# An attention and feed-forward block: which queue carries the maxima rows, the sums and the split weights, who computes the norm factors, and where the transposes stand

## The chip, the cores and the metric

The kernel runs on one core of a Trainium2 chip. Its time is the device time of one execution in microseconds. An execution can also be recorded by the hardware profiler, and every view quoted below comes from one such profiled execution. The engines have short names there: PE is TensorE's matmul row and PEld its weight loads, DVE is VectorE, ACT is ScalarE, POOL is GpSimd, SP is SyncE. A name that ends in q (SPq, ACTq, POOLq) is that engine's sequencer, which issues transfers.

## The reference

One transformer block on x of 2048 rows by 512 columns, with a modulation computed from a vector c:

```
mod = silu(c) @ w_mod                        # six vectors of 512: sa, ca, ga, sb, cb, gb
h = layernorm(x) * (1 + ca) + sa
q, k, v = split(h @ wqkv)                    # 32 heads of 16 columns
o = softmax(q k^T / 4) v                     # per head, 2048 by 2048 scores
x = x + ga * (o @ wo)
h = layernorm(x) * (1 + cb) + sb
x = x + gb * ((silu(h @ w_gate) * (h @ w_up)) @ w_down)      # 1792 hidden columns
```

All of it is float32. The kernel keeps that precision by splitting an operand into a rounded high part and a low rest and adding three products: high by high, high by low, low by high.

## The kernel before

The work falls into three stages. In the first, the rows of x are normalized, modulated, turned and multiplied with wqkv; queries and keys go to the DRAM buffers `qd` and `kd` in parts, and the values stay in `v_flat`. The second is the attention loop with most of the rest of the block laid into it. The third finishes what is left after the last score.

**Units and steps.** The 2048 queries are four chunks of 512, the 32 heads are eight groups of four. A *unit* is one chunk with one group, so there are 32 units, and every eight units end a chunk. A unit has 16 *steps*, one for each tile of 128 keys; the loop has 512 steps. In a step `score` (L496) runs once per head: one matmul of 128 keys by 512 queries into a PSUM bank and an exp on ScalarE into one of 13 tiles `pt_`. The product with the values, `pv_step` (L506), is done in two halves of 256 columns per step and follows the scores some steps later; it sums into one bank for the whole unit, and a column of ones in `v_flat` makes the row sums beside the products.

**Maxima.** The softmax needs each row's maximum before its scores are exponentiated. `max_one` (L466) computes the scores of a later unit once more in the other orientation and VectorE reduces each of these 128 by 512 results (L477). This runs 19 steps ahead of the scores (LEAD = 20), one such matmul beside each score matmul. When a unit's maxima are complete, `max_parts` (L479) joins and negates them on VectorE, and one step later `max_rows` (L488) turns them on TensorE, copies them on ScalarE and sends them as two extra rows into that unit's query operand `qop` with two transfers that ScalarE issues. They have to be there when the unit's first score starts.

**A unit's end.** `close_unit` (L816) runs when the last product of a unit has been issued, which is in the first step of the next unit. The output tile is copied from PSUM by ScalarE, in two halves inside plain steps. Then come, in order: `out_a` (the row sums go from the copied tile to the column tile `dn`), `out_b` two steps later (reciprocal on VectorE, then `dn` to DRAM), `out_r` three steps later (each head's row back from DRAM, repeated over 32 partitions, into `rb`), `out_c` four steps later (product on GpSimd, then to `o_dr`). All four transfers are on GpSimd's queue. At the end of a chunk `begin` loads its x and the output projection's weights at once, `load_o` (L647) fetches the chunk's outputs at five steps and `split_o` splits them at six.

**Keys and queries.** Three key buffers `kop` and three query buffers rotate. `before` (L827) reloads the keys of the unit after next at step 0 of a unit (two transfers of 768 KB) and its queries at step 1 (two of 192 KB), on SyncE's queue.

**Filling.** `plain` (L895) runs steps in groups of three pairs of a score and a maximum matmul, each group followed by a share of the products with the values. `filled` (L908) runs two steps and lays twelve ticks of other TensorE work between their pairs, LONG and SHORT being the two patterns. For each of the first three chunks the order is: plain steps up to `STARTS[ci]`; the output projection in four filled groups; six plain steps during which `scaled` (L796) issues `norm_scale` and `normalize` piece by piece from a side generator; two filled groups without work of their own, each followed by eight transposes (`turned`, L682) and two `modulate`; and then the feed-forward jobs, each `gate_up` in two filled groups and each `down` in one. `norm_scale` (L661) finds 1/sqrt(variance) of four row tiles by four Newton steps on tiles of 128 by 4, on VectorE; `normalize` (L678) applies it on ScalarE. After the third chunk's norm, REST = 30 plain steps come before its jobs, and seven of its jobs (KEEP) are left for the third stage. The fourth chunk's block is done there as well, with the last unit's way through `out_a` to `load_o` ahead of its output projection.

**Weights.** `split_weights` (L572) loads the raw weights of wo, gate, up and down, scales and splits them on GpSimd, and stores the parts to DRAM. It advances by one piece at two of every five steps from the start of the loop (L855). Its loads and stores are on SyncE's queue, as are the later loads of the parts, `load_gu` (L637, one gate/up tile of 1 MB, one job ahead) and `load_wd`.

The order of the work is written out by hand: each engine and each queue takes its instructions in the order in which this program emits them, and waits are set where a tile's reader or writer requires it.

## Time and profile before

| | |
|---|---|
| median of three runs | 2095.19 us (2092.72 to 2097.70) |
| the profiled execution | 2095.88 us |
| its span | 2093.7 us |
| TensorE matmuls, share of the span | 94% |
| VectorE | 75% |
| ScalarE | 60% |
| GpSimd | 20% |
| granted clock of TensorE, mean | 0.958 |

A page of the profile gives such shares; a view of windows gives, for a stretch of time, how long an engine (or one line's instructions) was busy, how many instructions it had and what clock was granted. A view of groups has one row per line, engine and kind of operation, with the busy time, the mean of one in ns, and the idle time of the engine just before them with what ended it. The view in order of time has one row per instruction, with its start, its length, and in brackets the idle time before it and who ended it. The chain of waits follows the instruction that ended last back to what released it, step by step.

### The profile page before, as it was taken

The numbers are of one execution on the slowest core, as the hardware profiler recorded it, in microseconds if no ns is written. First come the engines' busy times: TensorE is split into PE (matmuls) and PEld (weight loads), VectorE is DVE, ScalarE is ACT, GpSimd is POOL, SyncE is SP. The second block draws the span as 40 slices with busy tenths as digits, with TensorE's granted clock in tenths as the row PEclk, the third lists the DMA queues.
The fourth block names the chain that finished last, engine by engine and source line by source line (L and its number), as shares of the span: only waits on it lengthen the run. The fifth ranks groups of instructions, "written<-read, shape, count | busy, mean of one in ns | idle before, by whom it ended". The sixth has DMA issues, their size and how long they took to land.

```text
span 2093.7 us, 40510 instructions
## 1 busy us (share of the span) xinstructions
PE 1960.2 (94%) x16836; PEld 1185.0 (57%) x16836; DVE 1579.0 (75%) x2663; ACT 1251.8 (60%) x2306; POOL 422.4 (20%) x463
## 2 busy tenths in 40 slices
PE   7999989999998999999999999999999999998798
PEld 5765434444455666665446666664454466666687
DVE  6468978889897888888887888887887988831333
ACT  4224767778766666666766666666766766673100
POOL 2001254442022111111202111111202011122321
PEclk9998989999998999999999999999998999999899
DMA  8773575665453344443443443433532334332542
GB/s 295 250 235 90 125 217 158 222 169 126 115 130 64 93 116 104 109 110 90 130 110 84 105 108 90 133 90 69 130 70 49 90 89 118 135 117 96 201 181 101
DMA packets 84924, 267.69 MB, mean 128 GB/s; under 512 B 16540, under 2 KB 29340, under 8 KB 64060
## 3 DMA queue, kind: packets, MB, share of 16 engines
q1 hardware_dynamic: 67012, 239.82, 42.0%
q0 software_dynamic: 16576, 24.76, 3.7%
q8 instruction: 132, 2.16, 0.4%
q10 hardware_dynamic: 1152, 0.52, 0.1%
q14 instruction: 52, 0.43, 0.1%
HBM read 201.85 MB, written 62.13 MB: 126 GB/s over the span
## 4 chain that ended last, share of the span: by engine, by line
PE 63%; DMA 12%; DVE 10%; issue 6%; ACT 4%; POOL 3%; ACTq 1%; SPq 0%; POOLq 0%; DVEq 0%
PE bank L517 16%; PE bank L707 14%; PE bank L502 13%; DMA dn<-o 8%; DVE mx L477 7%; PE bank L715 6%; PE bank L475 6%; PE bank L207 6%; DMA rb<-d_dr 1%; DMA mid<-in_B_w_gate 1%; ACTq L494 1%; POOL wgu L581 0%; PE bank L687 0%; POOL mid L761 0%; DMA d_dr<-dn 0%
## 5 line engine op out<-in xcount | busy, mean ns | idle before, releaser
L477 DVE TENSOR_REDUCE mx<-bank 128x1 f32<-128x512 f32 x2048 | 1310.2, 685 | 223.1 <-PE bank L475 174.6
L502 PE MATMUL bank<-qop,kop 50*128 50x512 f32 x2048 | 810.1, 447 | 50.3 <-ACT pt__6239 L504 2.2
L475 PE MATMUL bank<-kop,qop 48*128 48x512 f32 x2048 | 821.0, 452 | 31.8 <-DVE mx L477 30.0
L502 PEld LDWEIGHTS bank<-qop,kop 50*128 50x128 f32 x2048 | 369.5, 191 | 385.6 <-issue 79.1
L475 PEld LDWEIGHTS bank<-kop,qop 48*128 48x128 f32 x2048 | 365.2, 191 | 73.5 <-DVE mx L477 51.3
L707 PE MATMUL bank<-act,wgu 64*128 64x512 f32 x1872 | 306.4, 393 | 0.3 <-DVE m L759 0.2
L707 PEld LDWEIGHTS bank<-act,wgu 64*128 64x128 f32 x1872 | 204.6, 187 | 33.9 <-DVE m L759 3.3
L707 PE MATMUL bank<-wd,mid 64*128 64x512 f32 x912 | 154.4, 398 | 1.0 <-POOL mid L761 0.4
L760 POOL CAST mid<-m 128x512 fp32r<-128x512 f32 x56 | 34.3, 612 | 482.2 <-DVE m L759 203.8
L707 PEld LDWEIGHTS bank<-wd,mid 64*128 64x128 f32 x912 | 100.2, 188 | 19.3 <-DVE m L759 3.2
L753 ACT ACTIVATE th<-bank 128x512 f32<-128x512 f32 x56 | 33.5, 598 | 123.8 <-PE bank L715 123.8
L757 DVE SCALAR_TENSOR_TENSOR q<-th,bank 128x512 f32<-128x512 f32 x56 | 38.2, 682 | 82.4 <-ACT th L753 82.4
L529 POOL DMA_DIRECT2D dn<-o x32 | 22.7, 711 | 384.0 <-ACT o L523 182.7
L207 PE MATMUL bank<-hT,wqs 128*128 128x512 f32 x384 | 95.4, 399 | 3.6 <-DVE prt L366 2.4
L207 PEld LDWEIGHTS bank<-hT,wqs 128*128 128x128 f32 x384 | 70.4, 188 | 26.0 <-issue 5.9
L772 DVE TENSOR_TENSOR x<-bank,x 128x512 f32<-128x512 f32 x84 | 54.1, 683 | 31.0 <-PE bank L707 21.0
L761 POOL TENSOR_TENSOR mid<-m,mid 128x512 fp32r<-128x512 f32 x56 | 72.2, 1289 | 4.6
L715 PE MATMUL bank<-wd,mid 128*128 128x512 f32 x216 | 56.7, 419 | 12.5 <-DVE q L757 7.8
L545 POOL TENSOR_TENSOR on<-o,rb 128x512 f32<-128x512 f32 x32 | 41.0, 1282 | 135.4 <-DMA rb<-d_dr 135.4
L534 POOL DMA_DIRECT2D d_dr<-dn x32 | 18.2, 568 | 198.6 <-DVE dn L533 198.6
L715 PEld LDWEIGHTS bank<-wd,mid 128*128 128x128 f32 x216 | 43.0, 201 | 24.7 <-DVE q L757 8.3
L366 DVE TENSOR_TENSOR prt<-bank,prt 128x512 fp32r<-128x512 f32 x32 | 22.0, 689 | 45.0 <-ACT prt L364 43.0
(6258 smaller groups left out, 5286.1 us busy)
## 6 DMA issues: line engine op xcount, KB each, us to landing
wgu<-gu_dr SPq DMA_DIRECT2D x48, 1024.0 KB
kop<-kd SPq DMA_DIRECT2D x62, 768.0 KB
wd<-wd_dr SPq DMA_DIRECT2D x28, 1024.0 KB
gu_dr<-wgu SPq DMA_DIRECT2D x14, 1024.0 KB
qop<-qd SPq DMA_DIRECT2D x64, 192.0 KB
kd<-prt SPq DMA_DIRECT2D x16, 512.0 KB
qd<-prt SPq DMA_DIRECT2D x16, 512.0 KB
rb<-d_dr POOLq DMA_DIRECT2D x32, 256.0 KB, 5.0
```

The source lines that it names most:

```text
L207: nc.tensor.matmul(pt, lhs(a, k), rhs(b, k), start=(n == 0), stop=(n == 3 * nk - 1))
L475: nc.tensor.matmul(pm, qop[u][rows, s, qt * P:(qt + 1) * P], kop[u % 3][rows, s, kc * CW:(kc + 1) * CW], start=True, stop=True)
L477: nc.vector.tensor_reduce(mx[u][:, b, s, qt, kc:kc + 1], pm, op=ALU.max, axis=AX.X)
L502: nc.tensor.matmul(sp, kop[u % 3][rows, h // 2, kt * P:(kt + 1) * P], qop[u][rows, h // 2, :], start=True, stop=True)
L517: nc.tensor.matmul(pv[u][32 * h:32 * h + 32, cols], v_flat[:, e0:e0 + 32], p_[h][:, cols], start=(kt == 0 and half == 0), stop=(kt == 15), ...
L545: nc.gpsimd.tensor_mul(on, o, rb)
L707: nc.tensor.matmul(outs[e], lhs(e, a, k)[rows], rhs(b, k)[rows], start=(ph == 0 and j == 0), stop=(ph == 1 and j == z))
L715: nc.tensor.matmul(outs[e], lhs(e, a, k), rhs(b, k), start=(j == 0), stop=(j == z))
L757: nc.vector.scalar_tensor_tensor(q, th, 1.0, outs[0], op0=ALU.add, op1=ALU.mult)
L760: nc.gpsimd.tensor_copy(mid[:, 0, :], m32)
L761: nc.gpsimd.tensor_sub(mid[:, 1, :], m32, mid[:, 0, :].bitcast(F32))
L772: nc.vector.tensor_add(ch.x2[:, t, :], outs[e], ch.x2[:, t, :])
```

## The change

- The two transfers of the maxima rows move from ScalarE's to SyncE's queue.
- The transfers of `out_a`, `out_b` and `out_r` move from GpSimd's to SyncE's queue; the one of `out_c` stays on GpSimd's, one step later. For the last unit all are on ScalarE's queue, issued one behind the other, and the product is on VectorE.
- Keys and queries of the unit after next are both loaded at step 6 of a unit instead of steps 0 and 1. `begin`, `load_o` and `split_o` come 6, 7 and 9 steps after a chunk's end instead of 0, 5 and 6.
- The weights' loads and stores move from SyncE's to GpSimd's queue; a piece is advanced every fourth step, two raw loads are kept ahead, and stores are issued as soon as their tile is made.
- The output tile is copied in one piece in plain steps too, and what remains of a group's products after a unit's end is put off to the next group.
- `norm_scale` leaves three operations on VectorE and puts the other 18 on the engine it is given, GpSimd inside the loop; `normalize` is on GpSimd inside the loop. Both are issued at once ahead of nine plain steps (NORM).
- The 16 transposes of a chunk are laid four by four into the last four groups of three further plain steps, each with its `modulate`, in the banks that the maxima use.
- Projections start six, eight and four steps later (STARTS), REST falls from 30 to 24.
- In the third stage the kept gate/up jobs go ahead of the kept down jobs, 36 of their matmuls beside the last unit's sums and 36 ahead of the norm factors, which stay on VectorE there. One more tile is lent to a `mid` of the last kept job.
- An exp on a small tile is put at the end of the first stage.

```diff
-REST = 30
-STARTS = (141, 267, 399)
+REST = 24
+NORM = 9
+STARTS = (147, 275, 403)
...
     sm.finish()
+    nc.scalar.activation(pa.tile([P, 1], F32, name="warm1"), eps_t, AF.Exp)
...
-            nc.scalar.dma_start(qop[u][64 * b + KR:64 * b + KR + 2].bitcast(F32), mr[16 * b:16 * b + 16].bitcast(F32))
+            nc.sync.dma_start(qop[u][64 * b + KR:64 * b + KR + 2].bitcast(F32), mr[16 * b:16 * b + 16].bitcast(F32))
...
-        if kt == 15 and by_halves:
-            nc.scalar.copy(o_[u][:, cols], pv[u][:, cols])
-        elif kt == 15 and half:
+        if kt == 15 and half:
             nc.scalar.copy(o_[u], pv[u])
...
-        nc.gpsimd.tensor_mul(on, o, rb)
-        nc.gpsimd.dma_start(o_dr[ci, g], on)
+        mul.tensor_mul(on, o, rb)
+        eng.dma_start(o_dr[ci, g], on)
...
         def store(dst, w):
-            nc.sync.dma_start(dst, w.bitcast(F32))
+            nc.gpsimd.dma_start(dst, w.bitcast(F32))
...
+        srcs = [(wod[:, 2 * k:2 * k + 2, :], 2) for k in range(NK // 2)]
+        for m in range(NF // FG):
+            srcs += [(wgd[:, :, cols(m)], NK), (wud[:, :, cols(m)], NK), (wdd[:, m * FG:(m + 1) * FG, :], FG)]
+        ahead = [raw(*srcs.pop(0)) for _ in range(2)]
+        yield
+
+        def following():
+            if srcs:
+                ahead.append(raw(*srcs.pop(0)))
+            return ahead.pop(0)
...
             for _ in range(4):
-                nc.vector.tensor_mul(a, rs, rs)
-                nc.vector.tensor_mul(a, a, va)
-                yield
-                nc.vector.tensor_scalar(a, a, -0.5, 1.5, op0=ALU.mult, op1=ALU.add)
-                nc.vector.tensor_mul(rs, rs, a)
-                yield
-            nc.vector.scalar_tensor_tensor(self.rs2[:, 1], mv[:, :, 0], -1.0, rs, op0=ALU.mult, op1=ALU.mult)
+                eng.tensor_mul(a, rs, rs)
+                eng.tensor_mul(a, a, va)
+                eng.tensor_scalar(a, a, -0.5, 1.5, op0=ALU.mult, op1=ALU.add)
+                eng.tensor_mul(rs, rs, a)
+            eng.tensor_mul(self.rs2[:, 1], mv[:, :, 0], rs)
+            eng.tensor_scalar_mul(self.rs2[:, 1], self.rs2[:, 1], -1.0)
...
+        def turned(self, tp, k):
+            for t in range(4):
+                nc.tensor.transpose(tp[:, t * P:(t + 1) * P], self.rows(t)[:, k * P:(k + 1) * P], ident)
+            self.modulate(tp, k)
...
     def close_unit(u, i):
-        res[u] = out_a(u)
-        if u < NU - 1:
-            at(i + 2, lambda: res.__setitem__(u, out_b(u, *res[u])))
-            at(i + 3, lambda: res.__setitem__(u, out_r(u, *res[u])))
-            at(i + 4, lambda: out_c(u, *res.pop(u)))
-            if u % NG == NG - 1:
-                at(i, lambda: begin(u // NG))
-                at(i + 5, lambda: chunks[u // NG].load_o())
-                at(i + 6, lambda: chunks[u // NG].split_o())
+        if u == NU - 1:
+            res[u] = out_a(u, nc.scalar)
+            return
+        res[u] = out_a(u, nc.sync)
+        at(i + 2, lambda: res.__setitem__(u, out_b(u, nc.sync, *res[u])))
+        at(i + 3, lambda: res.__setitem__(u, out_r(u, nc.sync, *res[u])))
+        at(i + 5, lambda: out_c(u, nc.gpsimd, nc.gpsimd, *res.pop(u)))
+        if u % NG == NG - 1:
+            at(i + 6, lambda: begin(u // NG))
+            at(i + 7, lambda: chunks[u // NG].load_o(nc.gpsimd))
+            at(i + 9, lambda: chunks[u // NG].split_o())
...
-        if 1 <= u and u + 2 < NU:
-            if kt == 0:
-                load_k(u + 2)
-            if kt == 1:
-                load_q(u + 2)
+        if kt == 6 and 1 <= u and u + 2 < NU:
+            load_k(u + 2)
+            load_q(u + 2)
...
-        if 0 <= i < UG - 4 and i % 5 in (0, 2):
+        if 0 <= i < UG and i % 4 == 3:
             next(weights2, None)
...
+        if by_halves:
+            most, owed = most + owed, 0
         while most and halves and 4 * halves[0][0] + 8 <= done:
             i, half = halves.pop(0)
-            pv_step(i, half, by_halves)
+            pv_step(i, half)
+            most -= 1
             if i % 16 == 15 and half:
                 close_unit(i // 16, done // 4 - 1)
-            most -= 1
+                if by_halves:
+                    break
+        if by_halves and most and halves and 4 * halves[0][0] + 8 <= done:
+            owed = most
...
-        side.append(scaled(ch))
-        plain(2 * WIN)
-        run(side.pop())
-        for kk in range(NK // 2):
-            filled(none, iter(()), ch.turned(outs, kk))
+        scaled(ch)
+        plain(NORM)
+        plain(WIN, [lambda tp, k=k: ch.turned(tp, k) for k in range(NK)])
...
-    rest = whole(chp, chp.jobs)
+    rest = whole(chp, [j for j in kept if j[0] is gate_up] + [j for j in kept if j[0] is down])
...
+    on = out_b(NU - 1, nc.scalar, *res[NU - 1])
+    on = out_r(NU - 1, nc.scalar, *on)
+    out_c(NU - 1, nc.scalar, nc.vector, *on)
+    ch.load_o(nc.scalar, (NK - 1,))
     ch.split_o((NK - 1,), True)
-    take(rest, 12)
+    take(rest, 36)
     for t in range(4):
         out_terms(ch, t, banks[t], (NK - 1,))
         if t % 2:
             add_o(ch, t - 1, banks[t - 1:t + 1])
-    run(ch.norm_scale())
+    take(rest, 36)
+    ch.norm_scale(nc.vector)
...
```

More of the change, by code (lines that the diff above doesn't have):

```diff
@@ L609, in split_weights @@
             parts(w[:, 0], w[:, 1], t)
+            store(wd_dr[m], w)
             yield
[L611 to L614 removed]
     class Chunk:
@@ L748, in gate_up @@
             ch.load_wd(0)
-        ch.mid[f] = mid = tile_mid()
+        ch.mid[f] = mid = spare.pop(0) if spare and f == NF - 1 else tile_mid()
         def after():
@@ L785, in block_kernel @@
     chunks = {}
-    side = []
+    side, spare = [], []
     def begin(ci):
@@ L893, in end_steps, with plain @@
             ended += 1
-    def plain(steps):
+    def plain(steps, tails=()):
         nonlocal four, bank
@@ L902, in plain, with filled @@
                 pair_of()
-                if side:
-                    next(side[0], None)
+            if w >= 4 * steps // WIN - len(tails):
+                tails[w - 4 * steps // WIN](four())
             pvs((HALVES[(w - 2) % 4] if done > 8 else 0) + (w == 4 * steps // WIN - 1), True)
             end_steps()
-    def filled(places, work, tail=None, pairs=8):
+    def filled(places, work, pairs=8):
         nonlocal four, bank
@@ L919, in filled @@
         hook()
-        if tail:
-            run(tail)
         pvs(6, False)
-        hook()
     def two_of(u):
@@ L933, in block_kernel @@
     at(n - 24, begin_last)
-    at(n - 13, lambda: chunks[last].load_o(range(NK - 1)))
+    at(n - 13, lambda: chunks[last].load_o(nc.gpsimd, range(NK - 1)))
     at(n - 11, lambda: chunks[last].split_o(range(NK - 1)))
@@ L1012, in block_kernel @@
         ch.load_gu(f)
-    for kk in range(NK // 2):
-        run(ch.turned(banks[2 * kk:2 * kk + 2], kk))
-        hook()
-        take(rest, 12)
+    take(rest, 24)
+    for k in range(NK):
+        ch.turned(banks[k], k)
+        take(rest, 6)
     run(rest)
```

89 lines of the change are left out of this document (35 added, 54 removed).

## The prediction

> **What bounds the kernel now.** I read the page first, then the time by stage, then inside a stage the instructions in order of time and the chain of waits. The sum below is made against the profiled execution, 2095.88 us, of which the span is all but 2.2 us; it stands 0.03% above the median of 2095.19.
>
> ```profile
> span 2093.7 us, 40510 instructions
> ```
>
> The attention loop has 512 score steps. A step is four score matmuls, each followed by one exp on ScalarE (L504), and, except in the last 19 steps, four maximum matmuls, each with one reduction on VectorE (L477). Four exps are one step, so the windows of line L504, cut where a stage begins, give time per step. Columns: window, length, ScalarE time of those exps with their count (up to two stray ones at the edges), granted clock, DMA.
>
> ```profile
> 187.59:588.84 401.25, 293.00 (x564) 0.91 0.59 157
> 588.84:619.52 30.68, 18.68 (x32) 1.00 0.56 112
> 619.52:662.95 43.43, 21.51 (x40) 0.80 0.14 54
> 662.95:976.85 313.90, 195.43 (x336) 1.00 0.45 110
> 976.85:1037.83 60.98, 49.70 (x96) 1.00 0.41 114
> 1037.83:1073.89 36.06, 18.64 (x32) 0.91 0.46 81
> 1073.89:1113.96 40.07, 21.48 (x41) 0.83 0.26 95
> 1113.96:1433.89 319.93, 195.38 (x337) 0.99 0.42 105
> 1433.89:1519.86 85.97, 62.19 (x121) 0.92 0.42 103
> 1519.86:1548.49 28.63, 18.78 (x32) 1.00 0.59 124
> 1548.49:1595.24 46.75, 21.46 (x40) 0.74 0.23 36
> 1595.24:1676.32 81.08, 62.09 (x121) 0.96 0.30 70
> 1676.32:1903.09 226.77, 145.66 (x257) 1.00 0.37 107
> ```
>
> In order these are: 141 plain steps (the weights are split beside them), then three times output projection (8 steps), norm block (10 steps, L661 to L696), feed-forward work (84, 84 and 64 steps) with plain stretches of 24, 30 and 30 steps between. Two quiet stretches show what a step costs when nothing is in its way:
>
> ```profile
> 382.30:408.55 26.25, 22.71 (x45) 1.00 0.73 284
> 789.27:832.23 42.96, 27.97 (x49) 1.00 0.40 111
> ```
>
> The first is 11 plain steps, 2.39 us each; the second 12 filled ones, 3.58 us each. So 225 plain steps (401.25 + 60.98 + 85.97 + 81.08 = 629.3 us) cost 92 us above 225 x 2.39 = 537.8; 30 steps of norm blocks (130.3) cost 59 above 71.7; 256 filled steps (956.0) cost 40 above 916.5. The kernel is bound by a step's work plus some 190 us of waits that return once per unit of 16 steps or once per norm block. Where they are thick the granted clock falls to 0.91 and 0.74, so each stall is paid again in slow matmuls.
>
> **The change part by part. Rows of maxima, ScalarE to SyncE.** Once per unit ScalarE issues two transfers itself:
>
> ```profile
> 543.88 1.31 ACTq L494 DMA_DIRECT2D qop<-mr  x2
> 545.23 0.60 ACT L504 ACTIVATE pt__5319<-bank 128x512 f32<-128x512 f32 x1 [1.38 <-PE bank L475]
> 545.88 0.18 PEld L502 LDWEIGHTS bank<-qop,kop 50*128 50x128 f32 x1 [1.09 <-ACT pt__5319 L504]
> L481 DVE TENSOR_REDUCE m<-mx 128x16 f32<-128x64 f32 x32 | 7.0, 217 | 0.8
> L483 DVE TENSOR_SCALAR nm<-m 128x16 fp32r<-128x16 f32 x32 | 9.5, 298 | 1.1
> L484 DVE SCALAR_TENSOR_TENSOR nm<-m,nm 128x16 fp32r<-128x16 f32 x32 | 6.6, 205 | 1.1
> ```
>
> For 1.31 us no exp starts, the two or three score banks fill, and TensorE stands 1.09 us. On SyncE the issue holds up no compute engine; behind it stand only key, query and weight loads, and the rows must land two steps later (4.8 us). The saving is 1.0 us per unit. What stays is the 0.72 us of VectorE (L481 to L484).
>
> By the Trainium skill, "DMA: Bandwidth & Descriptors", section "Issuing engines are not separate DMA queues", issuing from another engine saves only the issuing sequencer's time, usually small; the trace shows that time as 1.31 us here, and it is on the path.
>
> **Sums, GpSimd to SyncE, and the keys at the seventh step.** At a unit's end its sums go out as a column (dn), come back inverted (d_dr, rb), and VectorE's reciprocal (L533) stands in VectorE's order two steps after the issue. Today the next keys start just ahead:
>
> ```profile
> 547.39 1.98 SPq L401 DMA_DIRECT2D kop<-kd  x2
> 554.62 9.78 DMA dn<-o
> L533 DVE RECIPROCAL dn<-dn 128x16 f32<-128x16 f32 x32 | 8.0, 249 | 50.6 <-DMA dn<-o 50.6
> q1 hardware_dynamic: 427, 1.95, 94.8%
> rb<-d_dr POOLq DMA_DIRECT2D x32, 256.0 KB, 5.0
> L529 POOL DMA_DIRECT2D dn<-o x32 | 22.7, 711 | 384.0 <-ACT o L523 182.7 <-ACT o L521 172.0 <-ACT pt__13953 L504 16.1
> ```
>
> The queue's row is the DMA view of 962.0 to 975.2 us, one unit's keys and queries: 1.95 MB hold 16 engines 94.8% busy for 13.2 us. The 8 KB of dn issued into that take 9.78 us, the reciprocal waits (50.6 us in all), the reductions stand behind it and TensorE behind them. In the change dn is issued at step 1, d_dr after step 3, rb after step 4, and the keys only at step 6, behind all of them on SyncE's queue. With the keys away, dn should take between the 3.76 of a 256 KB copy in the tail (quoted below) and the present 9.78; I take 3 to 4, under the 4.8 us of two steps, so most of the 50.6 us goes; late next is then the step's own work. Its price is in the keys: they are needed at step 13 (the maxima run 19 steps ahead), so 7 steps, 16.7 us, stand against 13.2. In the plain stretch the weights, now on GpSimd's queue, keep some of the rest of the 0.59 DMA share: a unit took 45.5 us there, so 0.59 less 13.2/45.5 leaves 0.30, and 13.2/0.70 = 18.9 us is 2.2 us late. Bounds: 0, and turn for turn 26.4 - 16.7 = 9.7 us a unit. I take 1.0 us per unit of the weight stretch (nearer the first, as the weights use the engines only part of the time). In filled steps 7 x 3.58 = 25 us are there, but a gate/up load behind the keys can be late: four times 1.5 us, 6 us.
>
> GpSimd now issues the weights' 23 loads and 23 stores, at 0.71 us (L529) 33 us in the first 147 steps, and sheds its three issues per unit. Nothing waits for that: the first projection needs the weights at step 147 and they are split by step 95. Its product with rb (5.0 us to land) stands two steps, 4.8 us, after the issue; behind it stand splits and the feed-forward's casts, which have steps to spare, so it is costed at nothing; if that spare were gone, at the 0.2 us between.
>
> Copying the output tile at once and putting the next unit's first products off one group takes a wait of TensorE away; I leave it inside the residue below.
>
> **Plain steps after.** Per unit 16 x 2.39 = 38.2, plus 0.72 + 0.25 of VectorE and 0.5 for the rest, 39.7 us or 2.48 a step; with weights 2.54. There are 147 + 24 + 24 + 24 = 219: 147 x 2.54 + 72 x 2.48 = 552 us.
>
> **Norm block.** Now 20 small VectorE operations are strung between reductions, ScalarE waits in its order for the last of them, and the transposes come in a lump:
>
> ```profile
> 631.45 0.79 PE L502 MATMUL bank<-qop,kop 50*128 50x512 f32 x1 [2.17 <-ACT pt__6239 L504]
> L671 DVE TENSOR_TENSOR rs<-rs,mv 128x4 f32<-128x4 f32 x16 | 2.6, 163 | 0.5
> L679 ACT ACTIVATE mid<-x,rs,rs 128x512 f32<-128x512 f32 x12 | 9.7, 808 | 4.9 <-DVE rs L676 4.9
> L761 POOL TENSOR_TENSOR mid<-m,mid 128x512 fp32r<-128x512 f32 x56 | 72.2, 1289 | 4.6
> L727 DVE TENSOR_TENSOR x<-bank,x 128x512 f32<-128x512 f32 x12 | 7.7, 681 | 0.0
> L731 DVE BATCH_NORM_STATS2 stt<-x 128x6 f32<-128x512 f32 x12 | 8.1, 672 | 0.0
> 647.64 1.89 PE bank L687 x8
> ```
>
> The change leaves three small operations on VectorE, puts 18 and the four normalizations on GpSimd, gives them 9 plain steps (21.5 us), and lays four transposes into each of the next four groups. GpSimd has no such small operation in this trace. From below it is VectorE's 0.163, from above the 1.289 us of a full tile: 18 x 0.163 + 4 x 0.8 = 6 us, or 22 x 1.289 = 28 us. I take twice VectorE's, 9 us: the operands are as small as that row's. It is hidden by the nine steps; at the upper end it would be 7 us late per block, 20 in all, since the transposes wait, and on TensorE's order all scores behind them. The block after is 12 x 2.39 + 2 x (0.681 + 0.672) + 0.5 + 16 x 0.24 (eight in 1.89) + 1.5 = 37.2, and 1 us until the first gate/up has its input: 38.2, three times 115 us.
>
> **Filled steps after.** 16 x 3.58 + 1.0 = 58.3 a unit, 3.64 a step. 168 feed-forward steps 612 against 633.8, 24 projection steps 87 against 95.4, the last 64 lose 2: -32, plus the 6 above, -26.
>
> **Tail and start.**
>
> ```profile
> PE bank L742 <- ACT kop L655: 6.0, 1, 6.0
> PE bank L715 <- DVE q L757: 7.8, 1, 7.8
> 1907.17 5.36 DMA dn<-o
> 1926.26 3.76 DMA kop<-o_dr
> 186.30 1.28 ACT L504 ACT_TABLE_LOAD   x1
> ```
>
> The sums' chain of the last unit, 1907.17 to 1930.0 (23 us), is followed by the norm chain, both with too little TensorE work beside them. The change issues the first on ScalarE at once, multiplies on VectorE (0.69 for 1.30), and puts 36 gate/up matmuls beside each. I expect 4 and 2 us left of 13.8 plus some clock: -12 (from -3, if ScalarE's tanh behind its own transfers holds the banks, to -18). The early exp takes the 1.28 us table load off the first score: -1.3.
>
> **Sum.** Plain and norm blocks 759.6 to 552 + 115 = 667: -92 (225 + 30 and 219 + 36 are both 255 steps). -92 - 26 - 12 - 1.3 = -131; 2095.9 - 131 = **1965 us**.
>
> **The rivals. Shared engines.** The sums are late for want of DMA, and whose queue issues them is no cure; in the weight stretch they meet GpSimd's stores instead of the keys. For it: dn already sat on a queue of its own and still took 9.78 us. Against: it sat there behind 13 us of keys, which are gone from that place. Then half of the plain gain (77 us without the blocks) and half of the filled one stay away: 1965 + 38 + 13, about 2016 us.
>
> The skill's same page, section "Queues, rings and completion order", says that an engine takes turns between queues packet by packet; by this the weights would slow the sums at any place. The row above speaks against fair turns: 8 KB would not have needed 9.78 us.
>
> **One line for everything.** The slower case: on SyncE's single queue d_dr waits for the reciprocal, rb for d_dr, and the keys for both. If dn is as late as now, the reciprocal slips two steps, rb's issue with it, and the keys start at step 9: 4 steps, 9.6 us, for 13.2 plus rb's 5. That is 9 us late, with clock 11 us. It pays from 131/14 = 9.4 us in each of some 14 plain units; at 11 there and 2 to 3 in each of the 15 filled ones it is 190 us, so 2155 us. For it: three waits in a row at the head of one queue. Against: dn's cause goes by the same edit.
>
> **Norm factors not hidden.** The upper end above, with slow matmuls behind: 1965 + 20 + 10 = 1995 us.
>
> **More than that.** If the residues of 1.5 a unit shrink to 0.5 and the tail is closed: 1965 - 30 - 6, about 1930 us.
>
> **How the numbers follow.** Forecast 0.58 (own range 1940 to 1988), shared engines 0.20, norm factors late 0.09, more 0.06, one line 0.07. The range 1935 to 2035 leaves out the last and the edges. What can be told from no change is about 0.2%, 4 us. Only the one-line case is slower, 0.07; a partial form of it could end within the 0.2%, 0.02; faster 0.91.
>
> **What would show it.** Right: the first 147 steps under 380 us at a clock over 0.96; the reciprocal's wait for dn under 12 us in all; no DMA issue on ScalarE in the loop; norm blocks of 12 steps near 37 us with GpSimd's factors done before the first transpose; less than 8 us of TensorE waiting in the tail. Wrong: maximum matmuls (L475's line) waiting for kop for more than 10 us in all means the keys are late; scores waiting for qop that the rows are; reciprocals still waiting in the first stretch that the engines are shared; transposes waiting on GpSimd that the factors are not hidden.

## The result, and the profile after

| | before | after |
|---|---|---|
| median | 2093.95 us (2085.84 to 2097.70) | 1972.99 us (1964.96 to 1985.65) |
| the profiled execution | 2095.88 us | 1970.09 us |
| its span | 2093.7 us | 1968.3 us |
| granted clock of TensorE, mean | 0.958 | 0.982 |

The ratio of after to before, run on the same chip, is 0.943 with a 95% interval of 0.937 to 0.949. The medians lie 121 us apart, the profiled executions 126; the prediction was 131 us and 1965 us. The forecast held, and no rival came about. Not all of its reasons held, though, and the runs below are mostly about those.

The page's head and first part, of the kernel after, with busy times and shares of the span:

```profile
span 1968.3 us, 40520 instructions
PE 1892.3 (96%) x16836; PEld 1170.6 (59%) x16836; DVE 1567.9 (80%) x2614; ACT 1240.7 (63%) x2284; POOL 408.2 (21%) x476
```

Nearly the same work stands in a span 125.4 us shorter. The windows below hold the exps alone (line L506 after the change) and are cut where a stage begins, as in the prediction; columns: window, length, ScalarE time of those exps with their count, granted clock, DMA share, GB/s.

```profile
188.03:565.20 377.17, 304.57 (x588) 0.97 0.61 168
565.20:594.03 28.83, 18.80 (x33) 1.00 0.54 124
594.03:628.51 34.48, 25.17 (x49) 0.95 0.20 38
628.51:939.21 310.70, 195.72 (x337) 0.99 0.44 115
939.21:1006.08 66.87, 49.86 (x96) 0.95 0.47 110
1006.08:1034.88 28.80, 18.78 (x33) 1.00 0.54 124
1034.88:1070.07 35.19, 25.17 (x49) 0.95 0.20 36
1070.07:1375.59 305.52, 195.63 (x337) 1.00 0.44 118
1375.59:1442.48 66.89, 49.84 (x97) 0.92 0.47 110
1442.48:1471.29 28.81, 18.79 (x33) 1.00 0.52 125
1471.29:1505.79 34.50, 25.17 (x49) 0.95 0.20 39
1505.79:1564.44 58.65, 49.58 (x97) 1.00 0.32 66
1564.44:1787.65 223.21, 145.69 (x256) 1.00 0.38 118
```

In order: 147 plain steps, then projection (8 steps), norm block (12), jobs (84), 24 plain steps, and so on twice more; the last norm block is followed by 24 plain steps and 64 filled ones. Summed by kind, beside the windows of before:

| | before | after | moved by | predicted |
|---|---|---|---|---|
| up to the first exp | 187.6 | 188.0 | +0.4 | -1.3 |
| plain steps and norm blocks (255 steps) | 759.5 | 673.8 | -85.8 | -92 |
| filled steps (256) | 956.0 | 925.9 | -30.1 | -26 |
| after the loop | 190.6 | 180.7 | -10.0 | -12 |
| the span | 2093.7 | 1968.3 | -125.4 | -131 |

What is left of waiting stands in the table of waits (engine and line, what it waited for: us in total, times, longest):

```profile
PE bank L504 <- DMA qop<-mr: 20.6, 4, 6.4
...
DVE dn L534 <- DMA dn<-o: 8.8, 1, 8.8
```

The reciprocal waited 50.6 us before, 19 times, 10.5 us of it in the last unit; now it waits once, in the last unit, where nothing covers it. The maximum matmuls, which the prediction's list named next, have one wait of 1.4 us for a query load in the same table and none for keys. What is new is the first row: four times the scores wait for the rows of maxima, three of them for about 6 us, each time in the second unit after a chunk's end.

### The profile page after: what moved, and what is told of

The parts are those of the page before. It is cut to its first block, busy times and chain, and to the rows that moved or that the text cites. A ratio compares the mean times of both kernels' runs of the same rounds, so it can differ in the third digit from the quotient of the medians.

```text
span 1968.3 us, 40520 instructions
## 1 busy us (share of the span) xinstructions
PE 1892.3 (96%) x16836; PEld 1170.6 (59%) x16836; DVE 1567.9 (80%) x2614; ACT 1240.7 (63%) x2284; POOL 408.2 (21%) x476
## 4 chain that ended last, share of the span: by engine, by line
PE 66%; DVE 24%; DMA 6%; ACT 2%; POOL 1%; issue 1%; SPq 0%; POOLq 0%; ACTq 0%; DVEq 0%
DVE mx L479 23%; PE bank L713 18%; PE bank L519 15%; PE bank L504 13%; PE bank L208 7%; PE bank L721 7%; PE bank L477 6%; DMA qop<-mr 2%; DMA rb<-d_dr 1%; DMA wgu<-gu_dr 1%; DMA qop<-qd 1%; PE bank L161 0%; PE bank L695 0%; DMA wm_ab<-in_w_mod 0%; DMA wd<-wd_dr 0%
## 5 line engine op out<-in xcount | busy, mean ns | idle before, releaser
L504 PE MATMUL bank<-qop,kop 50*128 50x512 f32 x2048 | 780.6, 436 | 32.4 <-DMA qop<-mr 20.6
L477 PE MATMUL bank<-kop,qop 48*128 48x512 f32 x2048 | 794.2, 441 | 6.4 <-DVE mx L479 3.9
L504 PEld LDWEIGHTS bank<-qop,kop 50*128 50x128 f32 x2048 | 360.6, 187 | 339.0 <-issue 82.4
L477 PEld LDWEIGHTS bank<-kop,qop 48*128 48x128 f32 x2048 | 356.5, 187 | 42.1 <-DVE mx L479 18.8
L721 PE MATMUL bank<-wd,mid 128*128 128x512 f32 x204 | 50.3, 398 | 7.8 <-DMA wd<-wd_dr 6.5
L365 ACT CAST prt<-bank 128x512 fp32r<-128x512 f32 x32 | 18.8, 587 | 59.6 <-PE bank L208 46.5
L765 DVE TENSOR_TENSOR m<-bank,q 128x512 f32<-128x512 f32 x56 | 38.7, 691 | 20.5 <-PE bank L721 18.4
L713 PE MATMUL bank<-wgu,act 64*128 64x512 f32 x288 | 48.5, 396 | 0.5 <-issue 0.5
```

The lines of the kernel that those rows point to most:

```text
L477: nc.tensor.matmul(pm, qop[u][rows, s, qt * P:(qt + 1) * P], kop[u % 3][rows, s, kc * CW:(kc + 1) * CW], start=True, stop=True)
L504: nc.tensor.matmul(sp, kop[u % 3][rows, h // 2, kt * P:(kt + 1) * P], qop[u][rows, h // 2, :], start=True, stop=True)
L713: nc.tensor.matmul(outs[e], lhs(e, a, k)[rows], rhs(b, k)[rows], start=(ph == 0 and j == 0), stop=(ph == 1 and j == z))
L721: nc.tensor.matmul(outs[e], lhs(e, a, k), rhs(b, k), start=(j == 0), stop=(j == z))
L765: nc.vector.tensor_mul(m32, outs[1], q)
```

## The experiments

Two theories of the sums ran through the prediction without being told apart. *Keys*: the sums were late because the next unit's keys stood in front of them, and they are in time now because the keys come after. *Shared engines*: the DMA engines are too busy, whoever issues. The first also has two readings. Either the keys come later because the program writes them at step 6, or because they stand behind the sums in one queue.

Each ratio below is to the kernel before, run on the same chip as the experiment. The four runs of the kernel after lie between 1965 and 1986 us, so a difference of 13 or 14 us between medians is near the least that can be told; there the waits in the profile have to bear it out. No run puts the transposes back into a lump or the third stage back into its old order, so what these two are worth by themselves is not shown.

### Sums back on GpSimd's queue

```diff
-        res[u] = out_a(u, nc.sync)
-        at(i + 2, lambda: res.__setitem__(u, out_b(u, nc.sync, *res[u])))
-        at(i + 3, lambda: res.__setitem__(u, out_r(u, nc.sync, *res[u])))
+        res[u] = out_a(u, nc.gpsimd)
+        at(i + 2, lambda: res.__setitem__(u, out_b(u, nc.gpsimd, *res[u])))
+        at(i + 3, lambda: res.__setitem__(u, out_r(u, nc.gpsimd, *res[u])))
```

> The changed kernel with the sums' three transfers per unit (dn, d_dr, rb) issued by GpSimd again; keys stay at step 6. Theory 'keys': the sums were late only because the keys were started ahead of them; without keys there, GpSimd's queue does as well: reciprocal's wait for dn under 10 us, time 1965 to 1985. In the weight stretch, where GpSimd's own stores stand ahead in its order, up to 10 us more is possible. Rival 'queue': it is SyncE's queue that makes them early; then the wait returns to 30 to 50 us and the time to 2010 or more.

Measured: 2056.8 us, ratio to before 0.983 (0.979 to 0.987). Of the 121 us, 84 are gone again. From the table of waits:

```profile
DVE dn L534 <- DMA dn<-o: 73.6, 18, 9.0
```

SyncE's issues at the end of a unit (start, length, what):

```profile
537.20 2.31 SPq L402 DMA_DIRECT2D kop<-kd  x2
```

And GpSimd's, with the idle time before each and who ended it:

```profile
544.84 0.71 POOL L530 DMA_DIRECT2D dn<-o  x1 [24.52 <-ACT o L523]
555.53 0.56 POOL L535 DMA_DIRECT2D d_dr<-dn  x1 [9.98 <-DVE dn L534]
```

And the chain of waits, with the time until the sums landed:

```profile
544.84 10.12 DMA dn<-o
```

The keys are still written at step 6, and yet they are issued at 537.20, 7.6 us *before* the sums of the unit that has just ended. Nothing on SyncE's queue holds them any more: its sequencer ran ahead of the compute engines, as far as its waits were met. So the sums went out into 13 us of keys again, as in the kernel before. "Keys only at step 6" was read as a time, and it is none; the theory that GpSimd's queue would do as well missed.

The units of this one kernel can be compared too. Of the 31 units whose sums GpSimd issued, 21 had keys issued in the 8 us before, and there the 8 KB took 7.0 to 11.3 us to land; in the ten others they took 2.1 to 3.9 us. Sums and keys are on two queues here, so it is not the order in one queue that delays the sums but the keys under way on the shared DMA engines.

For the size: the first 147 steps, by windows of the exps as above, took 407.4 us against 377.2, which is 30 us. The rest lies in the later plain steps, the norm blocks and the filled steps (9, 20 and 32 us in the profiled executions, which lie 92 us apart). GpSimd now waits in its order for the copied tile and for the reciprocal, 24.52 and 9.98 us in the rows above. In the filled steps its casts for the feed-forward stand behind such waits: TensorE waits for a cast (`mid`) 15.5 us in two places, against 2.2 us in the kernel after. How much of the 32 us this explains was not taken apart.

The Trainium skill, "DMA: Bandwidth & Descriptors", section "Queues, rings and completion order", lets each DMA engine turn between queues packet by packet. Read as equal turns, this would bring the 8 KB of the sums through soon. The trace does not bear that reading out: they took 10.12 us with the bulk on SyncE's queue under way. How large a turn is, no run here shows.

### Keys and queries early again

```diff
-        if kt == 6 and 1 <= u and u + 2 < NU:
-            load_k(u + 2)
-            load_q(u + 2)
+        if 1 <= u and u + 2 < NU:
+            if kt == 0:
+                load_k(u + 2)
+            if kt == 1:
+                load_q(u + 2)
```

> The changed kernel with keys at step 0 and queries at step 1 as before; the sums stay on SyncE's queue. Theory 'keys': dn stands behind 13 us of keys in one line, the reciprocal's wait returns to 40 us or more over the loop, and the time to 2020 to 2060. Rival 'queue': the time stays under 1985.

Measured: 2016.6 us, ratio 0.964 (0.960 to 0.968). The same wait, in the table of waits:

```profile
DVE dn L534 <- DMA dn<-o: 58.7, 19, 8.8
```

All sums are on SyncE's queue here, and keys and queries are the only thing moved. The wait is at least as large as before the change (49.8 us in the loop against 40.2), as the theory said; the time fell 3 us short of its range. A general load on the DMA engines does not explain the sums: in the kernel after, the engines are busy too (a share of 0.61 in the first 147 steps), and without the keys ahead the sums are in time. Most of the loss, 35 us, is in the first 147 steps (412.1 us).

### The step alone, in the kernel before

The kernel before, with its keys and queries written at step 6 and nothing else changed:

```diff
-        if 1 <= u and u + 2 < NU:
-            if kt == 0:
-                load_k(u + 2)
-            if kt == 1:
-                load_q(u + 2)
+        if kt == 6 and 1 <= u and u + 2 < NU:
+            load_k(u + 2)
+            load_q(u + 2)
```

> The kernel before with one edit alone: keys and queries of the unit after next both at step 6. Theory 'keys': the reciprocal's 50.6 us for dn fall under 15 us and the time to between 2035 and 2060 (2094 less about 45, with slow clock that goes with it). In the weight stretch the keys now stand behind up to 3 MB of weight stores on SyncE's queue and some can be late at step 13, which takes up to 15 us of it back. Rival 'queue': under 10 us of gain, 2085 or more.

Measured: 2087.5 us, ratio 0.998 (0.996 to 1.000), no difference that can be told. From the table of waits:

```profile
DVE dn L533 <- DMA dn<-o: 39.4, 10, 10.4
```

And SyncE's issues of the keys, in two units:

```profile
546.07 1.99 SPq L401 DMA_DIRECT2D kop<-kd  x2
...
729.11 0.32 SPq L640 DMA_DIRECT2D wgu<-gu_dr  x1
729.48 0.90 SPq L401 DMA_DIRECT2D kop<-kd  x2
```

In the first unit the keys went out at 546.07 where they had gone out at 547.39, still ahead of the sums: six steps later in the program moved nothing. In the second they left behind a gate/up load that stands ahead of them on SyncE's queue, 3.9 us after the sums (725.59), where they had gone out 6.8 us before them. So it went in 14 of the 29 units that load keys: there a load or store of weights stood directly ahead of them in the queue. The sums took 2.3 us to land where no keys were ahead and 8.1 us where they were (medians). The edit as such sets no time; what stands ahead in the queue does. The reciprocals waited 11 us less than in the kernel before, and the time hardly shows it: the theory's 2035 to 2060 us missed, and its rival's 2085 or more came about.

### Sums and keys together on GpSimd's queue

```diff
...
-    def load_k(u):
-        load_parts(kop[u % 3], kd, u % NG, 0, S)
-
-    def load_q(u):
+    def load_k(u, eng=nc.sync):
+        load_parts(kop[u % 3], kd, u % NG, 0, S, eng)
+
+    def load_q(u, eng=nc.sync):
...
-        res[u] = out_a(u, nc.sync)
+        res[u] = out_a(u, nc.gpsimd)
...
-            load_k(u + 2)
-            load_q(u + 2)
+            load_k(u + 2, nc.gpsimd)
+            load_q(u + 2, nc.gpsimd)
```

> The changed kernel with the sums' three transfers and, from the third unit on, the keys and queries all on GpSimd's queue, in the same order (sums first, keys at step 6). Theory 'order in one queue': a place in the program is no time; SyncE has nothing else to do and issues keys as soon as their buffer is free, at step 0, unless something ahead of them in the same queue holds them back. With sums and keys on one queue again, whichever it is, the sums come first: reciprocal's wait for dn under 20 us in all (73.6 with the sums alone on GpSimd's queue). The time is 1980 to 2030, since keys now also stand behind GpSimd's splitting in the first stretch. Rival 'SyncE's queue is served better': dn stays late, 50 us or more of wait, and the time is 2040 or more.

Measured: 1991.6 us, ratio 0.952 (0.944 to 0.960), against 2056.8 with the sums alone on that queue. From the table of waits:

```profile
PE bank L477 <- DMA qop<-qd: 39.7, 9, 7.4
...
DVE dn L534 <- DMA dn<-o: 8.8, 1, 8.8
```

GpSimd's issues at a unit's end:

```profile
525.99 0.71 POOL L540 DMA_DIRECT2D rb<-d_dr  x1 [1.43 <-DMA d_dr<-dn]
526.69 1.16 POOL L402 DMA_DIRECT2D kop<-kd  x2
```

The keys leave 0.7 us after the sums' last transfer because they stand behind it, and the sums are never late in the loop. This settles the reading: sums and keys on *one* queue, sums first, keep the keys off the engines until the sums are through; which queue it is does not matter. The other wait, for the queries that follow the keys, is this version's price. Weights, sums and keys now share a queue, the keys come late to the maximum matmuls, and the first 147 steps take 410.7 us instead of 377.2. After them this kernel is the faster one, by 9 us of span (33.5 lost and 24.1 in all); its table of waits has no row for the rows of maxima.

### Weights on SyncE's queue

```diff
-            nc.gpsimd.dma_start(t.rearrange("p e c -> p (e c)").rearrange("p (k c) -> p k c", k=k), src)
+            nc.sync.dma_start(t.rearrange("p e c -> p (e c)").rearrange("p (k c) -> p k c", k=k), src)
...
-            nc.gpsimd.dma_start(dst, w.bitcast(F32))
+            nc.sync.dma_start(dst, w.bitcast(F32))
```

> The changed kernel with the weights' loads and stores on SyncE's queue again, in the places of the change. Theory 'order in one queue': a store waits at the head of SyncE's queue until GpSimd has split its tile, and keys, sums and rows of the first 141 steps stand behind it; reciprocal's wait for dn and scores' wait for rows come back there, the first 147 steps take 395 to 430 us instead of 377 and the whole 1990 to 2025. Rival 'engines': what counts is the load on the 16 engines, which is the same; then within 10 us of 1973.

Measured: 1986.3 us, ratio 0.950 (0.945 to 0.955), 13 us slower than the change and between what the two theories gave. From the table of waits:

```profile
PE bank L477 <- DMA qop<-qd: 18.9, 5, 5.9
```

The kind of wait was expected wrongly. Neither sums (8.8 us, in the last unit alone) nor rows got worse (19.5 for 20.6); the keys and queries did, five times, at step 13 of a unit, where they are first used. The first 147 steps take 393.9 us. Weights ahead of the keys on one queue make the keys late, as in the run above. So the move of the weights to GpSimd's queue is worth about 13 us (the intervals of the two ratios overlap, but the first 147 steps alone are 16.7 us longer here), and it is worth it through the keys and queries, which the prediction charged with 1 us per unit in this place and which are now in time.

### Rows of maxima back on ScalarE

```diff
-            nc.sync.dma_start(qop[u][64 * b + KR:64 * b + KR + 2].bitcast(F32), mr[16 * b:16 * b + 16].bitcast(F32))
+            nc.scalar.dma_start(qop[u][64 * b + KR:64 * b + KR + 2].bitcast(F32), mr[16 * b:16 * b + 16].bitcast(F32))
```

> The changed kernel with the maxima rows' two transfers issued by ScalarE again; all else as changed. Theory 'line': in the changed kernel scores wait 20.6 us for these rows in four units because the rows stand behind keys, x and projection weights on SyncE's queue. Then with their own queue that wait falls below 5 us, while ScalarE's 1.3 us issue is paid again in 31 units (about +1 us each): 1973 - 20 - 8 of slow clock + 31 = about 1976, between 1965 and 1990. Rival 'engines': the rows are late because the 16 DMA engines are busy, whatever the queue. Then the wait stays near 20 us and the issue comes on top: 1995 to 2010.

Measured: 2001.3 us, ratio 0.956 (0.951 to 0.960): 28 us for 32 units, 0.9 each where the prediction had 1.0, although the waits for late rows are 5 us shorter here. The run also asks whether the new wait for the rows comes from SyncE's queue. Table of waits:

```profile
PE bank L504 <- DMA qop<-mr: 15.6, 3, 5.6
```

With the rows on ScalarE's own queue the three long waits are still there, a little shorter. A fuller queue is not their cause; the rival, busy engines, had forecast this and its time. What lies in front of them shows in SyncE's issues of the kernel after, at the first chunk's end (start, length, engine, line, out<-in):

```profile
519.80 0.34 SPq L535 DMA_DIRECT2D d_dr<-dn  x1
521.81 0.56 SPq L540 DMA_DIRECT2D rb<-d_dr  x1
522.47 0.90 SPq L402 DMA_DIRECT2D kop<-kd  x2
523.42 1.44 SPq L402 DMA_DIRECT2D qop<-qd  x2
524.90 0.46 SPq L639 DMA_DIRECT2D x<-in_A_x  x1
525.59 0.84 SPq L644 DMA_DIRECT2D wgu<-wo_dr  x2
545.23 1.34 SPq L496 DMA_DIRECT2D qop<-mr  x2
```

Here the sums hold the keys (d_dr after the reciprocal, rb after d_dr, then keys at once), just as the prediction's order had it. But at a chunk's end x and the projection's weights follow the keys, and the chunk's outputs come on GpSimd's queue; the rows are issued at 545.23, and TensorE goes on at 554.67 (the idle time in brackets):

```profile
554.67 0.76 PE L504 MATMUL bank<-qop,kop 50*128 50x512 f32 x1 [6.39 <-DMA qop<-mr]
...
921.62 0.50 PE L713 MATMUL bank<-wd,mid 64*128 64x512 f32 x2 [1.99 <-POOL mid L766]
...
1811.60 1.22 PE L748 MATMUL bank<-kop,kop 128*128 128x512 f32 x2 [4.13 <-ACT kop L664]
...
1837.86 0.77 PE L721 MATMUL bank<-wd,mid 128*128 128x512 f32 x1 [6.46 <-DMA wd<-wd_dr]
```

The other three lines are in the last unit of a chunk and in the tail. The second and the last are taken up below; the third is the last unit's sums, left as it is.

### A chunk's x and projection weights behind the rows

```diff
-        chunks[ci] = ch = Chunk(ci, x2, act, hT)
+        chunks[ci] = Chunk(ci, x2, act, hT)
+
+    def begin_loads(ch):
         ch.load_x2()
...
             at(i + 9, lambda: chunks[u // NG].split_o())
+            at(i + 13, lambda: begin_loads(chunks[u // NG]))
```

> The changed kernel with a chunk's x and output projection weights (3 MB on SyncE's queue) loaded 13 steps after the chunk's end, behind the maxima rows, instead of 6. Theory: these 3 MB and the attention outputs' loads, right behind 13 us of keys, are what makes the rows late at the three chunk ends. The wait for rows falls from 20.6 us to under 6 and the time by 15 to 30 us, to 1943 to 1958. Rival: the keys alone or the outputs' loads make them late; then less than 8 us of gain, or the projection waits for its weights instead.

Measured: 1953.1 us, ratio 0.934 (0.929 to 0.940), 20 us faster than the change. From the table of waits:

```profile
PE bank L504 <- DMA qop<-mr: 2.2, 1, 2.2
```

SyncE's issues at the same place:

```profile
547.11 1.34 SPq L496 DMA_DIRECT2D qop<-mr  x2
548.49 0.41 SPq L639 DMA_DIRECT2D x<-in_A_x  x1
```

The rows now stand ahead of the bulk on the same queue, and the wait goes from 20.6 to 2.2 us. The three waits after chunk ends (6.39, 5.98 and 5.61 us) are gone; the one left stands in an early unit, as in the kernel after. The bulk alone does not do it: with the keys early, and the bulk where the change has it, the scores wait for rows 1.7 us in all. It takes the keys and the bulk one behind the other. So *shared engines* was right about the rows: the DMA engines were too full for them, on whichever queue. What cures it is again the order, small before bulk.

### Norm factors on VectorE, normalization on ScalarE

```diff
-        ch.norm_scale(nc.gpsimd)
+        ch.norm_scale(nc.vector)
...
-            ch.normalize(t)
+            ch.normalize(t, True)
```

> The changed kernel with the norm factors inside the loop on VectorE and the four normalizations on ScalarE again, issued at once as in the change; the transposes stay four by four in ordinary groups. Theory 'engine': 17 more small operations on VectorE (about 2.8 us) and four normalizations of 0.8 us that hold the exps until the factors are there cost 5 to 8 us per block with slow clock: 1973 to between 1985 and 2000. Rival 'lumps': the block was dear because of the transposes in a lump and the groups without work; then the engine of the factors is worth little, 1970 to 1980.

Measured: 1997.3 us, ratio 0.955 (0.950 to 0.960): 24 us, 8 per norm block. TensorE in order of time, with the idle time before the row:

```profile
602.86 0.79 PE L504 MATMUL bank<-qop,kop 50*128 50x512 f32 x1 [8.64 <-ACT pt__6339 L506]
```

One such gap stands in each block (8.64, 8.60, 8.59 us). The exps queue on ScalarE behind four normalizations that wait for VectorE's factors, and the scores wait for the exps. On GpSimd nothing of the scores stands behind this wait. The run moves the factors and the normalizations together, so it does not say what either costs alone.

### The output copy in halves, the next products not put off

```diff
...
-        if kt == 15 and half:
+        if kt == 15 and by_halves:
+            nc.scalar.copy(o_[u][:, cols], pv[u][:, cols])
+        elif kt == 15 and half:
             nc.scalar.copy(o_[u], pv[u])
...
-                if by_halves:
-                    break
```

> The changed kernel with the output tile copied in two halves again and the next unit's first products in the same group, in plain steps. Theory: TensorE waits for the copy about 1 us in each of some 17 unit ends inside plain steps, and 0.5 us of it was in the old step: 1973 to between 1983 and 1995. Rival: the wait is hidden behind the reductions, which bound plain steps; then under 5 us.

Measured: 1987.1 us, ratio 0.949 (0.943 to 0.955). Table of waits:

```profile
PEld bank L519 <- ACT o L523: 18.6, 32, 1.4
```

It is 4.9 us in the kernel after. The next unit's first products wait for the copy that frees their bank, on TensorE's order ahead of scores; 13.7 us more of this wait, and 14 us more in the median. The prediction had this gain, without a number, inside the 0.5 us per unit left for the rest.

### No early exp

```diff
-    nc.scalar.activation(pa.tile([P, 1], F32, name="warm1"), eps_t, AF.Exp)
```

> The changed kernel without the small exp at the end of the first stage. Theory: the table load of 1.28 us comes back ahead of the first score and with it the slow clock that followed it in the kernel before (13.65 us at half speed, about 5 us of work): 1973 to 1977 to 1982, and the first four steps take 12 us instead of 9. Rival: the slow clock there had another cause; then 1 us.

Measured: 1972.5 us, ratio 0.943 (0.936 to 0.949), the same as the change. The 1.28 us load is back in front of the first exp, but the loop loses nothing that these runs can tell. The first four steps take 10.1 us at a granted clock of 0.83, against 8.9 at 1.00 in the kernel after and 12.2 at 0.61 in the kernel before. So a part of the slow clock came back with the load, and the theory's 5 us did not. It stays open whether the 1.3 us of the prediction are there.

### Three of the remaining waits taken away

The edit of the chunk's loads, and two more: `out_c` two steps later except at a chunk's end, and the last w_down tile loaded early into a free half of a key buffer.

```diff
...
-        at(i + 5, lambda: out_c(u, nc.gpsimd, nc.gpsimd, *res.pop(u)))
+        at(i + (5 if u % NG == NG - 1 else 7), lambda: out_c(u, nc.gpsimd, nc.gpsimd, *res.pop(u)))
...
+    w6 = kop[(NU - 3) % 3][:, 1, :].rearrange("p (b f d) -> p b f d", b=2, f=FG)
+    chp.wd[NF // FG - 1] = w6
+    nc.sync.dma_start(w6.bitcast(F32), wd_dr[NF // FG - 1])
...
```

> As the kernel with x and projection weights loaded 13 steps after a chunk's end, and two more edits: the product with rb and its transfer two steps later where no chunk ends, so that GpSimd's casts for the feed-forward no longer stand behind a wait for rb; and in the tail the last down weights of the third chunk are loaded into a free half of a key buffer as soon as it is free, ahead of the gate/up loads. Expected beyond the former: the 6.4 us wait for wd in the tail and the 2 us wait in unit 15 with its slow clock go: 8 to 16 us more, 1930 to 1945.

Measured: **1937.5 us** (1929.1 to 1943.4), ratio 0.926 (0.921 to 0.932), 35 us faster than the change and the fastest of all. Its granted clock is 0.990. The two extra edits answer the second and the last of the four TensorE waits shown above: 1.99 us behind a cast, and 6.46 us for the last w_down tile, which has no row in this kernel's table of waits any more. The first of them is GpSimd's order in the last unit of a chunk, in the kernel after:

```profile
917.33 1.29 POOL L546 TENSOR_TENSOR on<-o,rb 128x512 f32<-128x512 f32 x1 [25.91 <-DMA rb<-d_dr]
920.35 0.60 POOL L547 DMA_DIRECT2D o_dr<-on  x1 [1.73 <-DVE mx L479]
920.95 0.62 POOL L766 CAST mid<-m 128x512 fp32r<-128x512 f32 x1
```

The cast that a `down` needs stands behind the product and its transfer, which wait for `rb`. Two steps later the product no longer stands in its way. Which of the two edits brought how much of the 16 us beyond the run above was not taken apart.

## Why the prediction was right, and where it was not

**Sums and keys.** The place was right (40 of the 50.6 us of reciprocals waiting stood in the loop and are gone; the list allowed 12 in all, and 8.8 are left, in the last unit), and so was the cause, the keys. The step "the keys only at step 6, behind all of them on SyncE's queue" holds two reasons, and only the second does the work. As a place in the program the sixth step is no time: in the kernel before it put the keys behind the sums in half of the units and left the ratio at 0.998, and with the sums on GpSimd and the keys at step 6 the time was 2057 us. As a place behind the sums on one queue it holds the keys in every unit. The sum came out because the change has both. Had the prediction costed the two edits apart, it would have given the wrong one a gain.

**Shared engines** was wrong in its forecast, as the sums are in time beside the weights. Its mechanism is real: keys under way on another queue make the sums late (7.0 to 11.3 us to land against 2.1 to 3.9 within one run), and the same happens to something it was not said of, the rows at three chunk ends.

**Rows.** The 1.0 us per unit was 0.9. The clause that "the rows must land two steps later (4.8 us)" was left standing without a price; it failed where keys, x, projection weights and outputs run at once, for 18.0 of the 20.6 us of waiting. The unit after a chunk's end is a place that the prediction did not cost: its quiet stretches (382 and 789 us) lie in the middle of chunks.

**Plain steps.** The first 147 took 377 us against 373, and the list asked for under 380 at a clock above 0.96 (0.97). The other 72 took 192.4 against 179: two of the three late rows lie there (66.9 us twice, 58.7 in the third, against 59.5 each). With the norm blocks this is the term most out of size, and in the other direction. Keys were charged 1 us per unit in the weight stretch and cost next to nothing (1.4 us of waiting, once).

**Norm blocks.** 34.5, 35.2 and 34.5 us against 38.2, better than forecast. GpSimd's groups (busy us, mean ns):

```profile
L678 POOL TENSOR_TENSOR rs<-rs 128x4 f32<-128x4 f32 x12 | 2.4, 196 | 48.2 <-DVE rs L676 47.5
L690 POOL TENSOR_SCALAR mid<-x,rs,rs 128x512 f32<-128x512 f32 x12 | 9.1, 769 | 0.3
```

A small operation costs 0.196 us, near VectorE's 0.163 and far under the twofold price that was taken; with four normalizations of 0.769 a block needs 18 x 0.2 + 3.1 = 6.7 us where 9 was estimated. Nothing waits for it: in the first block the last normalization ends at 604.2 and the first transpose starts at 619.4.

**Filled steps.** -30 against -26. The gate/up loads late behind the keys, priced at 6 us, cost one wait of 0.45 us. `out_c` "costed at nothing" cost 2 us in one unit: the work said to hide it, casts "which have steps to spare", had none in a `down`.

**Tail.** -10 against -12. The list asked for less than 8 us of TensorE waiting; it is 4.13 and 6.46. The sums' chain kept its 4 us as forecast. The other is a new wait that was not foreseen: with gate/up ahead of down, the last w_down tile is loaded behind the gate/up loads into the one buffer that is free late.

**Start.** The 1.3 us can't be told from nothing.

So -131 was too large by 6: plain steps 18 us worse than forecast (4 and 14), norm blocks 11 better, filled steps 4 better, tail and start 4 worse; the terms are rounded.

## What to carry to other kernels

A transfer's place in the program is an order in its queue and not a time: a queue whose waits are met runs ahead, so put the small urgent transfer ahead of the bulk one *on the same queue* and let its waits hold the bulk back. Then look at the place where the bulk is thickest, here a chunk's end, and ask which small transfer stands behind it there. What stands behind a wait on an in-order engine is worth a step or two of distance, even on an engine that is 21% busy.

## What the hardware showed that was not expected

A queue of its own does not protect a small transfer. With the sums alone on GpSimd's queue and keys under way on SyncE's, the 8 KB took up to 11.3 us to land, and the reciprocal waited in 17 units of the loop, up to 5.1 us. In the tail of the kernel after, with no keys left to load, the chain of waits has the same 8 KB at less than half of that:

```profile
1791.47 3.92 DMA dn<-o
```

A stall is followed by slow matmuls. All engines behind the wait after the first chunk's end (window, length, PE busy, PEld, DVE, ACT, POOL, granted clock, DMA share, GB/s):

```profile
554.60:558.00 3.40, 3.33 (x18) 1.74 (x20) 1.89 (x3) 1.57 (x3) 3.21 (x4) 0.50 0.00 0
558.00:561.50 3.50, 3.50 (x28) 1.45 (x24) 1.94 (x4) 2.19 (x5) 0.00 (x0) 0.56 0.00 0
561.50:565.00 3.50, 3.50 (x44) 1.51 (x40) 3.48 (x6) 3.06 (x6) 0.00 (x0) 1.00 0.04 7
```

For some 6 us after a wait of 6.39 the clock is about half. By the Trainium skill, "TensorE: Matmul & The Clock Gate", section "What's actually happening", the clock is halved after an idle window of about 3.4 us and released after a busy one, in windows that run freely. The trace agrees: 0.50 and 1.00, and 0.56 where a window of the view straddles the change. The whole price of a late row, by the run that took three of them away, was 19.9 / 3 = 6.6 us, where the waits were 5.6 to 6.4. That is less than the wait and the slow stretch together, so the prediction's remark that "each stall is paid again in slow matmuls" is not borne out here as a price on top of the wait.
